# Second chunk's maxima as 16-bit parts made on VectorE, and products in column halves, in the first batch of an mLSTM and Fourier kernel

## Chip, cores and metric

The kernel runs on one core of one Trainium2 chip. The metric is device time in microseconds (us) of an execution of the whole program. The engines are named as the profile names them: PE is TensorE (matrix products, with PEld its weight loads), DVE is VectorE, ACT is ScalarE, POOL is GpSimd, and SP issues DMAs.

## What is computed

An mLSTM cell (batch 4, 8 heads, 768 steps, head size 40) feeds a Fourier mixing layer with a two-layer network. The part that matters here is the recurrence and its running maximum `m`:

```python
for t in range(S):
    kt, vt, qt = (k[:, :, t], v[:, :, t], q[:, :, t])
    m_new = np.maximum(f_gate[:, :, t] + m, i_gate[:, :, t])
    f_stab = np.exp(f_gate[:, :, t] + m - m_new)
    i_stab = np.exp(i_gate[:, :, t] - m_new)
    m = m_new
    C = f_stab[:, :, None, None] * C + i_stab[:, :, None, None] * np.einsum('bhd,bhe->bhde', vt, kt)
    n = f_stab[:, :, None] * n + i_stab[:, :, None] * kt
    h_tilde = np.einsum('bhde,bhe->bhd', C, qt)
    nq = np.einsum('bhd,bhd->bh', n, qt)[:, :, None]
    denom = np.maximum(np.abs(nq), 1.0)
    o = 1.0 / (1.0 + np.exp(-o_gate[:, :, t]))
    y[:, :, t] = o * h_tilde / denom
...
X = np.fft.fft(x, axis=1)
X = np.fft.fft(X, axis=2)
mixed = np.real(X).astype(np.float32)
u = x + mixed
mu = np.mean(u, axis=-1, keepdims=True)
var = np.mean((u - mu) ** 2, axis=-1, keepdims=True)
un = (u - mu) / np.sqrt(var + 1e-06)
ch = np.maximum(un @ w_ch1, 0.0) @ w_ch2
```

## The kernel before

The sequence of 768 steps is cut into six chunks of 128. Inside a chunk the recurrence becomes matrix products: scores of queries and keys (`ps`, line 587), each weighted by an exponential of gate values, then products with the values (`hb`), and a state `C` carried from chunk to chunk (`pc`). Batch 0 is done chunk by chunk, six chunks, while the weights of the network are loaded and converted; batches 1 to 3 run in half chunks among the network's products of the batch before. After its chunks, batch 0 goes through folds on DVE and POOL (lines 892 to 904), the Fourier products over the sequence (`pz`, `hb`, line 970) and over features (`pu`, line 1004), and then into the network.

There is no planner with costs: the order of instructions on each engine is the order in which the program issues them. The function `gates` issues the work of the first microseconds line by line (lines 277 to 302); everything later is put into a plan by slot and phase (`at(slot, phase, ...)`) and is issued in the order of these keys. Engines run their queues in order and wait for each other by semaphores.

What `gates` does for the maxima: the gate arrays are held as 32 rows (batch and head) by chunk and step. `sums` scans the forget gate (`F`), `maxima` subtracts it from the input gate (`a`), copies the carries (`shift`), scans the running maximum (`M`), and makes `nM` and `m_in` of it. This is done for chunk 0 (`first`) and then for chunks 1 to 5 in one go (`others`), all on DVE. `columns` turns `a` (and on a second call `wk`, the weights made by ACT) by PE transposes into columns; both go to one PSUM tile `hb`, and DVE copies them to `colT`.

The exponentials of a chunk need the maximum of each head along the free axis on all 128 partitions. `spread_max` makes them in PSUM for four heads at a time: first a product of the bf16 identity with a triangular mask of large numbers (line 228), then for each head a product that spreads one row (line 233). For chunks 0 and 1 this is an fp32 product of a column of the 128-wide identity with the 128 rows of `Mq` or `M`, so that the rows above 32 have to be zero (line 188). For chunks 2 to 5 it is a bf16 product: `parts` (lines 239 to 243, on POOL) splits each fp32 maximum into three bf16 numbers that add up to it, `M3`, stacked on 96 rows, and `sel` is a stack of three bf16 identities. `mlstm_exp` (line 556, ACT) reads the result. `spread_decay` (line 258) spreads the decays `g`, made by ACT in `decay` (line 267), in the same way in fp32 to the tile `pG`, which DVE multiplies with the queries (`qg`, line 564).

`idle_products` (line 143) are products of zeros whose result nobody reads: three at the start, and two in slot 17, before the folds' products.

## Time and profile before

| | us |
|---|---|
| median of 3 runs | 383.57 |
| the three runs | 384.47, 383.57, 379.48 |
| the profiled execution | 382.09 |
| its span in the profile | 380.2 |

The profiled execution is a run of its own; the span is what the trace covers, 1.9 us less than the device time. All times in what follows are counted from the start of the span. The granted clock of PE is shown as 0.999 over the span. A row of the timeline has start, duration, engine, line, operation, output and inputs, shape, and the number of merged instructions; in brackets stands how long the engine had been idle, and who released it. A product in fp32 appears as two records, one in bf16 as one. A record of PE lasts some 0.2 us beyond the start of the next one, so the pace of products is read from the starts.

The records that belong to the changed lines:

| line, engine | what | records | median of one |
|---|---|---|---|
| 970 PE | `pz`, 128x386 f32 | 10 | 488 ns |
| 970 PE | `hb`, 64x386 f32 | 10 | 513 ns |
| 143 PE | `pi`, 128x256 f32 | 10 | 634 ns |

### The profile page before, as it was taken

How to read it: one execution, taken by the hardware profiler on the slowest of the kernel's cores; microseconds unless marked ns; L12 is line 12 of the kernel's file. 1: busy time of each engine (PE TensorE's matmuls, PEld its weight loads, DVE VectorE, ACT ScalarE, POOL GpSimd, SP SyncE). 2: the span in 40 equal slices, each digit the busy share in tenths (PEclk: the TensorE clock that was granted, in tenths of full speed). 3: DMA queues.
4: the chain of work that ended last, by engine and by line, in shares of the span. 5: the costliest groups of instructions: out<-in, count | busy, mean ns of one | idle time of the engine just before them, and what ended most of it. 6: DMA issues, size and time to landing. Idle time of an engine off the chain costs nothing.

```text
span 380.2 us, 11433 instructions
## 1 busy us (share of the span) xinstructions
PE 373.3 (98%) x4602; PEld 278.2 (73%) x4602; DVE 280.8 (74%) x662; ACT 171.4 (45%) x501; POOL 133.9 (35%) x240
## 2 busy tenths in 40 slices
PE   8999999999999999999999999999999999999996
PEld 6887655567677777666578999676488996546996
DVE  7788999999998585787964787987745885245552
ACT  4878757756442114764442153854520233544000
POOL 5568433775686124471501424561300000020000
PEclk9999999999999999999999999999999999999999
DMA  7978565999870428460002737300000001000011
GB/s 195 284 219 287 168 184 148 252 241 265 278 207 29 127 66 238 134 174 26 0 3 62 205 99 195 102 3 3 0 2 34 17 20 36 0 0 2 34 36 34
DMA packets 20500, 41.93 MB, mean 110 GB/s; under 512 B 3256, under 2 KB 9744, under 8 KB 20320
## 3 DMA queue, kind: packets, MB, share of 16 engines
q1 hardware_dynamic: 20448, 41.21, 37.5%
q8 instruction: 36, 0.59, 0.7%
q14 instruction: 16, 0.13, 0.1%
HBM read 37.10 MB, written 4.10 MB: 108 GB/s over the span
## 4 chain that ended last, share of the span: by engine, by line
PE 79%; DVE 9%; ACT 2%; issue 1%; SPq 1%; POOL 1%; DMA 0%; DVEq 0%; ACTq 0%; POOLq 0%
PE po L1346 22%; PE pm L1217 19%; PE po L1289 8%; PE pm L1134 7%; PE ph L587 5%; PE pm L1151 4%; PE ps L587 4%; PE pu L1004 3%; PE pz L958 2%; PE put L1053 2%; PE pzt L958 1%; PE hb L587 1%; DVE e L480 1%; DVE stats L1027 1%; DVE e L465 1%
## 5 line engine op out<-in xcount | busy, mean ns | idle before, releaser
L1295 DVE SCALAR_TENSOR_TENSOR x<-po,rstd,x 128x160 f32<-128x160 f32 (+1 forms) x69 | 27.1, 394 | 36.3 <-PE po L1346 33.0
L1223 DVE TENSOR_TENSOR h<-h,pm 128x384 f32<-128x384 f32 x60 | 30.5, 550 | 24.2 <-PE pm L1217 11.8
L583 POOL TENSOR_SCALAR_AFFINE_SELECT W<-W 64x512 f32<-64x512 f32 x36 | 28.1, 780 | 37.8 <-ACT W L556 28.8
L1217 PE MATMUL pm<-uT,w_sb 128*128 128x384 f32 x90 | 37.3, 503 | 0.1
L556 ACT ACTIVATE W<-W,colT 128x64 f32<-128x64 f32 x144 | 36.6, 336 | 1.6 <-DMA W<-M_d 1.6
L710 POOL TENSOR_TENSOR C<-C,decB 128x164 f32<-128x164 f32 x33 | 18.1, 549 | 49.4 <-DVE C L717 45.9
L1289 PE MATMUL po<-w_sb,h 128*128 128x320 f32 x120 | 33.6, 432 | 0.0
L1134 PE MATMUL pm<-uT,w_sb 64*64 64x384 f32 x320 | 32.0, 496 | 0.0
L1077 POOL TENSOR_TENSOR t<-rstd 128x6 f32<-128x6 f32 x12 | 3.7, 311 | 76.1 <-DVE v L1071 75.6
L568 POOL TENSOR_TENSOR qg<-qk,Gb 128x512 f32<-128x512 f32 x21 | 28.1, 1337 | 4.5 <-DMA Gb<-G_d 4.2
L1289 PEld LDWEIGHTS po<-w_sb,h 128*128 128x128 f32 x120 | 22.5, 190 | 8.9
L1151 PE MATMUL pm<-uT,w_sb 128*128 128x384 f32 x80 | 28.4, 496 | 0.0
L1346 PE MATMUL po<-T,S 128*128 128x160 f32 x180 | 27.8, 301 | 0.2 <-DVE x L1295 0.2
L1346 PEld LDWEIGHTS po<-T,S 128*128 128x128 f32 x180 | 25.4, 190 | 1.3 <-DVE x L1295 0.4
L1346 PE MATMUL po<-w_sb,h 128*128 128x160 f32 x180 | 26.3, 300 | 0.0
L1346 PEld LDWEIGHTS po<-w_sb,h 128*128 128x128 f32 x180 | 25.2, 190 | 1.4 <-DVE x L1295 0.3
L1217 PEld LDWEIGHTS pm<-uT,w_sb 128*128 128x128 f32 x90 | 15.7, 189 | 12.1 <-DVE h L1223 4.1
L1272 ACT ACTIVATE h<-h 128x384 f32<-128x384 f32 x45 | 23.1, 520 | 2.9 <-DVE h L1223 2.9
L1134 PEld LDWEIGHTS pm<-uT,w_sb 64*64 64x64 f32 x320 | 11.1, 132 | 15.5 <-issue 13.4
L574 POOL TENSOR_TENSOR vw<-kvt,colT 128x328 f32<-128x328 f32 x23 | 19.6, 852 | 7.0 <-DVE colT L290 2.7
L1151 PEld LDWEIGHTS pm<-uT,w_sb 128*128 128x128 f32 x80 | 14.3, 190 | 10.1 <-issue 1.2
L587 PE MATMUL ps<-qk 40*64 40x64 f32 (+1 forms) x768 | 19.9, 240 | 0.3 <-DVE C L717 0.3
(255 smaller groups left out, 825.2 us busy)
## 6 DMA issues: line engine op xcount, KB each, us to landing
kvt<-in_kv SPq DMA_DIRECT2D x24, 336.0 KB
qk<-in_qkT SPq DMA_DIRECT2D x48, 160.0 KB
raw<-in_w SPq DMA_DIRECT2D x10, 640.0 KB
W<-M_d SPq DMA_DIRECT2D x36, 128.0 KB
so<-in_o SPq DMA_DIRECT2D x24, 160.0 KB
out<-x SPq DMA_DIRECT2D x23, 160.0 KB
Gb<-G_d SPq DMA_DIRECT2D x42, 80.0 KB
ds_sb<-in_dft_s SPq DMA_DIRECT2D x1, 1158.0 KB
```

The source lines that it names most:

```text
L556: nc.scalar.activation(out=k.W[:, h, :], in_=M, func=AF.Exp, scale=-1.0, bias=colT[:, c, 0, b * H + h:b * H + h + 1])
L568: nc.gpsimd.tensor_tensor(out=k.qg[:, :, t], in0=k.qk[:, 0, :, t], in1=k.Gb[:, :, t], op=OP.mult)
L583: nc.gpsimd.affine_select(out=W, in_=W, compare_op=OP.is_ge, fill=0.0, base=base, pattern=[[0, H], [-1 if back else 1, LH]], channel_multi ...
L587: nc.tensor.matmul(out, w, x, start=start, stop=True, skip_group_check=True)
L1134: nc.tensor.matmul(banks[i][half(cols)], w1_rest(n)[half(i), half(cols)], u[half(i)], start=start, stop=not start, skip_group_check=True)
L1151: nc.tensor.matmul(k.pm[i], w1_block(ch, f // 2 * 2 + i), u[2 * ch], start=(ch == 0 and not ahead), stop=(ch == 1 and (ahead or n in (2, 5 ...
L1217: nc.tensor.matmul(bank, w, u, start=start, stop=True, skip_group_check=True)
L1223: nc.vector.tensor_tensor(out=h, in0=h, in1=bank, op=OP.add)
L1272: nc.scalar.activation(out=h, in_=h, func=AF.Relu, scale=-1.0)
L1289: nc.tensor.matmul(k.po[m], hidden(gr, f)[:, i * L:(i + 1) * L], w2_sb[:, f, :], start=(f == 0), stop=(f == NFF - 1))
L1295: nc.vector.scalar_tensor_tensor(out=u, in0=po, scalar=k.rstd[:, c:c + 1], in1=u, op0=OP.mult, op1=OP.add)
L1346: nc.tensor.matmul(po, a[:, f], w[:, f], start=start and f == 0, stop=f == half - 1, skip_group_check=True)
```

## The change

It has three parts. First, the maxima of chunk 1 are spread with bf16 products like those of chunks 2 to 5; their parts are made on DVE, right behind the scan of `others`, and the copy of the first chunk's weight columns (`colT[:, first, 1]`) now stands behind them instead of ahead of the scan. The zeros above row 32 of `M[:, 1]` are no longer written, and the zeros of `g` move from DVE to POOL. Second, the two masks of chunk 1 are issued ahead of the decay products, and the eight maxima behind them. Third, the idle products, batch 0's sequence products of line 970 and its feature products of line 1004 (not the row of its own) are issued in column parts: halves, and thirds for the idle ones of slot 17. On ACT and SP nothing changes place.

```diff
+    def columns_of(n, parts):
+        return [slice(i * n // parts, (i + 1) * n // parts) for i in range(parts)]
+
+    def idle_products(n, rest, at_=None, halves=1):
         pw = bank("pi", [L, 2 * L], at_)
         for i in range(n):
-            nc.tensor.matmul(pw, rest[:, 0:L], rest, start=True, stop=True, skip_group_check=True)
+            for cols in columns_of(2 * L, halves):
+                nc.tensor.matmul(pw[:, cols], rest[:, 0:L], rest[:, cols], start=True, stop=True, skip_group_check=True)
...
-        idle_products(3, rest)
+        idle_products(3, rest, halves=2)
...
-        nc.vector.memset(M[:, 1], 0.0)
...
+        nc.gpsimd.memset(g[:, 0:3], 0.0)
...
-        def spread_max(b, c, h0):
+        def spread_mask(b, c, h0):
...
+        def spread_max(b, c, h0):
+
+            k = chunks[b, c]
+            if c != 1:
+                spread_mask(b, c, h0)
             for h in range(h0, h0 + NP):
                 bh = b * H + h
-                w, x = (ident[:, bh:bh + 1], (Mq, M)[c][:, c, :]) if c < 2 else (sel[:, bh:bh + 1], M3[:, c, :])
-                nc.tensor.matmul(k.M[-1][:, h - h0, :], w.to_broadcast([w.shape[0], L]), x, start=False, stop=True,
+                w, x = (sel[:, bh:bh + 1], M3[:, c, :]) if c > 0 else (ident[:, bh:bh + 1], Mq[:, c, :])
+                nc.tensor.matmul(k.M[h0 // NP][:, h - h0, :], w.to_broadcast([w.shape[0], L]), x, start=False, stop=True,
                                  skip_group_check=True)
 
-        def parts(s):
+        def parts(s, eng=nc.gpsimd):
 
-            m, rest_ = (M if s.start == 2 else Mq)[0:BH, s], shift[:, s]
-            nc.gpsimd.tensor_copy(out=M3[0:BH, s], in_=m)
...
+            m, rest_ = (M if s.start < 3 else Mq)[0:BH, s], shift[:, s]
+            eng.tensor_copy(out=M3[0:BH, s], in_=m)
+            eng.tensor_tensor(out=rest_, in0=m, in1=M3[0:BH, s], op=OP.subtract)
+            eng.tensor_copy(out=below[:, s], in_=rest_)
+            eng.tensor_copy(out=M3[BH:2 * BH, s], in_=rest_)
+            eng.tensor_tensor(out=M3[2 * BH:, s], in0=rest_, in1=below[:, s], op=OP.subtract)
...
         mlstm_exp(0, 0, 0)
-        nc.vector.tensor_copy(out=colT[:, first, 1], in_=pt[:, first])
         mlstm_exp(0, 0, NP)
         maxima(others, M[0:BH, 0, L - 1:L])
+        parts(slice(1, 2), nc.vector)
+        nc.vector.tensor_copy(out=colT[:, first, 1], in_=pt[:, first])
         pt = columns(others, 0)
         mlstm_load_o(0, 1)
-        nc.vector.memset(g[:, 0:3], 0.0)
         nc.vector.tensor_copy(out=colT[:, others, 0], in_=pt[:, others])
         decay(slice(1, 2))
         weights(others)
-        spread_max(0, 1, 0)
-        spread_max(0, 1, NP)
+        for h0 in (0, NP):
+            spread_mask(0, 1, h0)
         spread_decay(0, 1)
+        for h0 in (0, NP):
+            spread_max(0, 1, h0)
         pt = columns(others, 1)
...
-        at(17, FILL_PE + 2.7, idle_products, 2, rest, 3)
+        at(17, FILL_PE + 2.7, idle_products, 2, rest, 3, 3)
...
-            nc.tensor.matmul(out, fe[:, p, fm], ds_sb[:, p, i], start=(p == TG - 1), **kw)
+            for cols in columns_of(NK, 2):
+                nc.tensor.matmul(out[:, cols], fe[:, p, fm], ds_sb[:, p, i, cols], start=(p == TG - 1 and cols.start == 0), **kw)
...
-            nc.tensor.matmul(o, z, t, start=(i == 0 or b == 0 and i == 3), stop=(i in (2, 4)), skip_group_check=True)
+            for cols in columns_of(o.shape[1], 2 if b == 0 and i < 3 else 1):
+                nc.tensor.matmul(o[:, cols], z, t[:, cols], start=(cols.start == 0 and (i == 0 or b == 0 and i == 3)),
+                                 stop=(i in (2, 4)), skip_group_check=True)
```

More of the change, by code (lines that the diff above doesn't have):

```diff
@@ L137 @@
     EVAC, FILL, MAIN, FILL_PE = range(4)
-    def idle_products(n, rest, at_=None):
+    def columns_of(n, parts):
+        return [slice(i * n // parts, (i + 1) * n // parts) for i in range(parts)]
+    def idle_products(n, rest, at_=None, halves=1):
         pw = bank("pi", [L, 2 * L], at_)
         for i in range(n):
-            nc.tensor.matmul(pw, rest[:, 0:L], rest, start=True, stop=True, skip_group_check=True)
+            for cols in columns_of(2 * L, halves):
+                nc.tensor.matmul(pw[:, cols], rest[:, 0:L], rest[:, cols], start=True, stop=True, skip_group_check=True)
     def gates(gp):
@@ L229, in spread_max @@
                              skip_group_check=True)
+        def spread_max(b, c, h0):
+            k = chunks[b, c]
+            if c != 1:
+                spread_mask(b, c, h0)
             for h in range(h0, h0 + NP):
                 bh = b * H + h
-                w, x = (ident[:, bh:bh + 1], (Mq, M)[c][:, c, :]) if c < 2 else (sel[:, bh:bh + 1], M3[:, c, :])
-                nc.tensor.matmul(k.M[-1][:, h - h0, :], w.to_broadcast([w.shape[0], L]), x, start=False, stop=True,
+                w, x = (sel[:, bh:bh + 1], M3[:, c, :]) if c > 0 else (ident[:, bh:bh + 1], Mq[:, c, :])
+                nc.tensor.matmul(k.M[h0 // NP][:, h - h0, :], w.to_broadcast([w.shape[0], L]), x, start=False, stop=True,
                                  skip_group_check=True)
-        def parts(s):
-            m, rest_ = (M if s.start == 2 else Mq)[0:BH, s], shift[:, s]
-            nc.gpsimd.tensor_copy(out=M3[0:BH, s], in_=m)
-            nc.gpsimd.tensor_tensor(out=rest_, in0=m, in1=M3[0:BH, s], op=OP.subtract)
-            nc.gpsimd.tensor_copy(out=below[:, s], in_=rest_)
-            nc.gpsimd.tensor_copy(out=M3[BH:2 * BH, s], in_=rest_)
-            nc.gpsimd.tensor_tensor(out=M3[2 * BH:, s], in0=rest_, in1=below[:, s], op=OP.subtract)
+        def parts(s, eng=nc.gpsimd):
[5 more added lines that the diff above has]
+            eng.tensor_tensor(out=M3[2 * BH:, s], in0=rest_, in1=below[:, s], op=OP.subtract)
         def queries():
```

## The prediction

> **What bounds the kernel now.** I read the page first (busy shares), then the chain of waits in order of time, then the timelines of PE and DVE around the change.

> ```profile
> span 380.2 us, 11433 instructions
> PE 373.3 (98%) x4602; PEld 278.2 (73%) x4602; DVE 280.8 (74%) x662; ACT 171.4 (45%) x501; POOL 133.9 (35%) x240
> ```

> PE is nearly always occupied, so whatever takes work or a wait off PE's queue early lets all that follows start earlier, unless another engine or a transfer comes last first. The chain of waits, followed back from the end, can be traced to 19.1 us:

> ```profile
> 19.11 0.11 DVE dec L320
> 19.23 0.04 issue
> 19.26 1.09 PE pG L258 x16
> ```

> From there it runs through PE to 24.3, DVE and POOL to 30.2, PE, ACT to 38.6, DVE nearly without a break to 60, a DMA stretch, and PE alone from about 78. What frees DVE at 19.1 is thus what starts everything after. The timeline of PE before it:

> ```profile
> 7.19 0.61 PE L228 MATMUL pM<-later_r,ident_b 128*128 128x512 bf16 x1
> 7.59 1.91 PE L233 MATMUL pM<-Mq,ident 128*128 128x128 f32 x8
> 9.43 1.76 PE L587 MATMUL ps<-qk 40*64 40x128 f32 x32
> 11.12 0.49 PE L273 MATMUL hb<-ident,a 32*128 32x32 f32 x5
> 11.54 0.39 PE L228 MATMUL pM<-later_b,ident_b 128*128 128x512 bf16 x1
> 11.77 1.05 PE L233 MATMUL pM<-M,ident 128*128 128x128 f32 x8
> 12.66 0.38 PE L228 MATMUL pM<-later_b,ident_b 128*128 128x512 bf16 x1
> 12.88 1.05 PE L233 MATMUL pM<-M,ident 128*128 128x128 f32 x8
> 13.86 1.09 PE L258 MATMUL pG<-x,ident 128*64 128x128 f32 x16
> 14.88 0.49 PE L273 MATMUL hb<-ident,x 32*128 32x32 f32 x5
> 18.04 0.39 PE L233 MATMUL pM<-M,sel 96*128 96x128 bf16 x4
> ```

> No wait stands between 9.43 and 17.9: here PE's own queue is the bound. And DVE in the same stretch:

> ```profile
> 7.29 0.19 DVE L290 COPY colT<-hb 128x32 f32<-128x32 f32 x1 [1.29 <-PE hb L273]
> 7.40 0.80 DVE L210 TENSOR_TENSOR a<-a,F 32x640 f32<-32x640 f32 x1
> 8.13 0.69 DVE L212 COPY shift<-F 32x5 f32<-32x5 f32 x1
> 8.86 1.54 DVE L213 TENSOR_TENSOR_SCAN M<-shift,M,a 32x640 f32<-32x640 f32 x1
> 10.80 0.38 DVE L295 MEMSET x<- 128x384 f32 x1
> 15.42 0.33 DVE L310 COPY colT<-hb 128x160 f32<-128x160 f32 x1 [2.25 <-PE hb L273]
> 15.66 0.48 DVE L465 TENSOR_SCALAR e<-raw 128x640 uint32<-128x640 uint32 x1
> ```

> DVE stands still for 1.29 us behind the column copy of line 290, and again for 2.25 us until PE's transposes of 14.88 are done. After that it is busy without a gap to 19.6, ending with qg of line 564 (18.44, 0.68), whose end frees the bank that PE's pG of 19.26 writes.

> **The products of the second chunk's maxima.** Before, 4 fp32 products take 0.89 us of PE (11.77 to 12.66, and again up to about 13.8). With the bf16 parts, 4 products are worth 0.23 (18.04 to the next mask at 18.27, all in the same PE clock). Two groups: 2 x 0.66 = 1.32 us. The gap of 0.09 between the last fp32 product and pG also goes, since pG now stands right behind the masks. New order from 11.54: two masks 0.45 (0.23 + 0.22), pG 1.02 (13.86 to 14.88), eight products 0.46; together 1.93 against 3.34 before. The transposes of 14.88 come at 13.47: **1.4 us earlier**.

> **The five DVE instructions added.** Their price on DVE is not in the trace for this form. Upper bound: the same five on POOL (line 239 on, 10.47 to 12.44), 1.97 us. Lower: DVE's copy of 32 columns (0.19) and its subtraction of 128 (0.28) give 3 x 0.19 + 2 x 0.28 = 1.1. I take 1.4, nearer DVE's own rows (its copy of 160 columns takes 0.33). They are paid by the scan's move: without line 290 ahead, the subtraction starts at 6.0, when the long sum of 4.54 (1.47) ends, not 7.40. That is 1.4 us earlier; the 0.69 of line 212, a copy of five values beside POOL's vw of 7.57, should shrink too, as vw now waits for the later column copy. I count 0.4. So the maxima are done at about 8.6 instead of 10.40, m_in at 9.0, the parts at 10.3, line 290's copy at 10.5. PE's transposes of 11.12 write the tile that this copy reads, and their wait for DVE is the last one ahead of the products, so it must cover the parts as well: ready 0.6 us early, cost nothing. With 1.97 it is 11.1, still just hidden. If that cover were gone, each microsecond of lateness would be one of the end.

> **What waits behind the later copy.** POOL's vw of the first chunk moves from 7.57 to about 10.6, its own parts for chunk 3 from 10.47 to about 11.7 (ending 13.7). They are wanted by PE at 18.04 less 1.4; vw is wanted by pc at 17.27 less 1.4. Hidden by two to four microseconds. No DMA issue moves on SP past another.

> **The masks ahead, the maxima behind pG.** ACT's exponentials of the chunk started at 12.98, right after its weights. Now decay can start when ACT is free at 10.7 instead of 11.21, but the maxima end at about 13.3, so the exponentials start 0.3 us later, and the chain behind them on ACT (copies, decays of 15.57 on, G_d's issue on SP at 16.88) ends 0.3 later, near 17.2. Who waits: DVE's weighing, at 17.01 less 1.4 = 15.6, its second half at 16.2, against exponentials done at 15.5: free. DVE's dec, at about 17.6: free. PE's heads copy on ACT, 17.48 before, now about 17.15, ahead of px at 20.71 less 1.4: free. The G_d write goes out late by 0.3, but the Gb loads behind it (21.25) feed POOL at 27.31, which DVE released, not they.

> **Memsets.** M's (0.17) leaves DVE before its first input lands; g's (0.38) leaves DVE and costs POOL about as much at 4.9, where POOL is idle until vw. Zero.

> **Column halves.** Ten transform products of 386 columns (line 970) and nine of 321 (line 1004) become two each; the idle ones two at 1.2 us and three at 41.0. In the same stage products of half the width take half the time: the two records of 193 columns of line 967 start 0.17 apart, those of 386 of line 970 0.33. Cost 0 to 0.1 per group of products, nothing taken; what there is hides while DVE is last: the pu products done by about 52.3 are first read by DVE's add at 53.11. Idle thirds: the transposes load 128 weight columns five times in 0.38 us (line 273), so under 0.08 each, near the 0.07 that a third of 0.22 streams. No cost. [...]

> **Sum.** -1.4 on PE's queue at 14.9; DVE's run 15.42 to 19.1 starts 1.4 earlier, with all its inputs there; pG of 19.26 at about 17.9. Everything on the chain after is started by what precedes it. The profiled execution took 382.09 for its span of 380.2, so it becomes 380.7. The median of the three runs is 1.48 higher, 383.57, and becomes 382.2. As the runs lie between 379.48 and 384.47, I put the forecast between the two: **381.4**.

> **Rivals.** *PE is fast earlier in other runs.* In this run the mask takes 0.61 at 7.19 and 0.39 at 11.54: PE went from half to full speed near 10.8. Were it fast from 8.4 on, PE would reach the transposes near 9.9 and wait: before, for the maxima (10.40), now for the parts (10.5). Then the old kernel has its transposes of x at 10.45 + 0.89 + 0.22 + 0.89 + 1.02 = 13.5 and the new one at 10.55 + 0.42 + 1.93 = 12.9: a gain of 0.6 only, 382.2 on the same footing. [...] Chance 0.22.

> *The gain is hidden.* A transfer between 19 and 60 comes last instead. SP's Gb issue of 21.25 stood 0.9 behind G_d's landing and won't move. Against it: POOL's 27.31 and DVE's 24 to 27 were released by engines. Time unchanged, 382.8. Chance 0.18.

> *Slower: the halves pay for their weights.* 19 more products are 38 more records between 42 and 58. If each let 0.1 of its 0.19 us load show, that is 3.8, of which 53.11 - 52.3 = 0.8 hides: +3.0 - 1.4 = +1.6, 384.4. It decides from about 0.06 per record. Against it: 180 records of 160 columns with loads of 190 ns run 0.136 apart (line 1346, x20 in 2.72). Chance 0.06.

> *It doesn't do what it says* (DVE's parts late, PE standing at 11.1): 382 to 383, within the second rival.

> **Numbers.** Forecast 0.50, rivals 0.22, 0.18 and 0.06, 0.04 for what I don't see (such as clock changes in the fold stage). The range of 8 in 10 takes the runs' scatter, some 2 us for a median, and the rivals: 378.6 to 384.2. About 2% (7.7 us) is what a measurement of this kernel can tell from no change; none of the cases reaches it: faster 0.04, within 0.93, slower 0.03.

> **What would show it.** Right: L213's scan near 7.1; five DVE instructions on 32x128 done before 10.6; eight bf16 products in about 0.5 behind pG; DVE's idle before L310 ending near 14; pG of chunk 3 near 17.9, and the same lead at the first products of batch 1 after 60. Wrong: a wait of PE on DVE near 11; ACT idle before the chunk's exponentials growing beyond 1 us; PE later at the transforms than the lead allows; the lead gone by 60.

## The result

Each kernel's time is the median of its executions; the ratio to the kernel before has a 95% interval.

| | median us | lowest to highest | executions |
|---|---|---|---|
| before | 382.93 | 379.48 to 384.47 | 6 |
| changed | 387.34 | 385.41 to 387.78 | 6 |

The ratio is 1.0152 [1.0116, 1.0189]: slower by 4.4 us between the medians, outside the predicted range of 378.6 to 384.2, on the side that had a chance of 0.03 beyond 2% and 0.06 as a rival. The ratios leave out executions over 1.5% above their kernel's fastest; since the cause found below puts executions there, the tables also give the median of all and how many ran with a lowered mean clock (under 0.998).

The profiled execution of the changed kernel took 387.16 us, 5.07 more than that of the kernel before. Its page begins:

```profile
span 385.1 us, 11524 instructions
PE 374.6 (97%) x4646; PEld 283.3 (74%) x4646; DVE 280.2 (73%) x665; ACT 171.5 (45%) x501; POOL 131.5 (34%) x241
```

PE is busy for 1.3 us more in a span that is 4.9 longer: most of the time was lost standing still. Below, "put products" are the products that write the tile `put`, one group for each batch; they mark how far the kernel has come. The timeline of DVE (start, duration, instruction, and in brackets the idle time before it with its releaser):

```profile
6.05 0.81 DVE L214 TENSOR_TENSOR a<-a,F 32x640 f32<-32x640 f32 x1
6.79 0.15 DVE L216 COPY shift<-F 32x5 f32<-32x5 f32 x1
6.98 1.54 DVE L217 TENSOR_TENSOR_SCAN M<-shift,M,a 32x640 f32<-32x640 f32 x1
...
8.71 0.21 DVE L249 CAST M<-M 32x128 bf16<-32x128 f32 x1
...
9.75 0.28 DVE L253 TENSOR_TENSOR M<-shift,below 32x128 bf16<-32x128 f32 x1
10.07 0.19 DVE L303 COPY colT<-hb 128x32 f32<-128x32 f32 x1
```

DVE does what was forecast, slightly sooner: the scan at 6.98, the five parts in 1.32 us (8.71 to 10.03), the column copy at 10.07. The timeline of PE:

```profile
7.40 1.10 PE L599 MATMUL ps<-qk 40*64 40x128 f32 x32
10.32 0.49 PE L283 MATMUL hb<-ident,a 32*128 32x32 f32 x5 [1.81 <-DVE colT L303]
...
11.28 1.76 PE L268 MATMUL pG<-x,ident 128*64 128x128 f32 x16
12.96 1.03 PE L243 MATMUL pM<-M,sel 96*128 96x128 bf16 x8
...
20.06 1.09 PE L268 MATMUL pG<-x,ident 128*64 128x128 f32 x16
```

In this execution PE runs fast from 4.7 us on (the clock records begin with a full clock at 4.72; the scores take 1.10, not 1.76, and are done at 8.5), so the transposes stand for 1.81 us behind the copy of line 303. Then PE is slow: pG takes 1.76 instead of 1.09. The decay products of chunk 3 start at 20.06, not at the forecast 17.9; before it was 19.26. The windows say why (columns: stretch, its length, busy time and count of PE, PEld, DVE, ACT, POOL, granted clock, DMA share, GB/s):

```profile
11.50:18.40 6.90, 6.90 (x81) 5.98 (x79) 3.82 (x7) 3.87 (x15) 5.07 (x10) 0.51 0.89 281
```

By the clock records of the trace, the half clock lasts from 11.55 to 18.37. This early loss of 0.8 us against the profile of before is not the 4.9. By the first put product it has shrunk to 0.27 (55.23 against 54.96), and the scores of 78.04 stood at 77.83 before. The comparison flatters the change, though, for in the profile of before the clock rose only at 10.83. In the halves-only run below, which has the old early part and a clock that rose at 4.54, chunk 3's decay products start like this:

```profile
17.05 0.66 PE L262 MATMUL pG<-x,ident 128*64 128x128 f32 x8 [0.39 <-DVE dec L324]
```

Its first put product stands at 52.75. At the same phase of the clock the changed kernel is thus 3.0 us late at chunk 3 and 2.5 late at put.

The other loss comes later. The changed kernel's chain of waits in order of time (start, duration, what) goes on so:

```profile
78.04 1.00 PE ps L599 x62
79.05 0.11 PE ph L599 x2
79.16 2.78 issue
81.94 0.67 PE ph L599 x27
82.61 6.40 PE pm L1166 x14
```

In the middle of 32 products of one group, PE stands for 2.78 us and waits for nothing that the profile shows: no engine, no transfer of data. In the kernel before, the same products run through:

```profile
78.67 0.68 PE L587 MATMUL ph<-kvt,W 64*64 64x41 f32 x31
```

Right behind the hole the granted clock is 0.50 again, from 83.23 to 86.64; 3.41 us at half the pace are worth 1.7, by an estimate from that clock. 0.2 + 2.8 + 1.7 is 4.7 of the 4.9. Some 0.6 us more are lost near 110 us and won back by 153, untraced. From the second group of put products on (146.89 against 141.37) to the end the two kernels need 238.2 and 238.8 us.

### The profile page after: what moved, and what is told of

Same layout as the page of the kernel before. It is cut to its first block, busy times and chain, and to the rows that moved or that the text cites. A ratio compares the mean times of both kernels' runs of the same rounds, so it can differ in the third digit from the quotient of the medians.

```text
span 385.1 us, 11524 instructions
## 1 busy us (share of the span) xinstructions
PE 374.6 (97%) x4646; PEld 283.3 (74%) x4646; DVE 280.2 (73%) x665; ACT 171.5 (45%) x501; POOL 131.5 (34%) x241
## 4 chain that ended last, share of the span: by engine, by line
PE 84%; DVE 9%; ACT 2%; issue 2%; DMA 1%; POOL 1%; SPq 0%; DVEq 0%; ACTq 0%; POOLq 0%
PE po L1361 22%; PE pm L1232 19%; PE po L1304 8%; PE pm L1149 7%; PE ph L599 5%; PE pm L1166 5%; PE ps L599 4%; PE pu L1018 3%; PE pz L970 2%; PE put L1068 2%; PE hb L599 1%; PE pzt L970 1%; ACT W L568 1%; PE pz L983 1%; DVE stats L1042 1%
## 5 line engine op out<-in xcount | busy, mean ns | idle before, releaser
L1232 PE MATMUL pm<-uT,w_sb 128*128 128x384 f32 x90 | 37.3, 503 | 0.1
L1166 PE MATMUL pm<-uT,w_sb 128*128 128x384 f32 x80 | 30.1, 521 | 0.0
L580 POOL TENSOR_TENSOR qg<-qk,Gb 128x512 f32<-128x512 f32 x21 | 26.9, 1283 | 6.9 <-DMA Gb<-G_d 6.6
L1232 PEld LDWEIGHTS pm<-uT,w_sb 128*128 128x128 f32 x90 | 15.7, 189 | 12.1 <-DVE h L1238 4.1
L1166 PEld LDWEIGHTS pm<-uT,w_sb 128*128 128x128 f32 x80 | 15.1, 199 | 10.8 <-issue 2.9
L1149 PEld LDWEIGHTS pm<-uT,w_sb 64*64 64x64 f32 x320 | 11.1, 132 | 15.5 <-issue 13.4
L586 POOL TENSOR_TENSOR vw<-kvt,colT 128x328 f32<-128x328 f32 x23 | 18.8, 818 | 6.3 <-DVE colT L303 5.2
```

Source lines behind the costliest of these rows:

```text
L580: nc.gpsimd.tensor_tensor(out=k.qg[:, :, t], in0=k.qk[:, 0, :, t], in1=k.Gb[:, :, t], op=OP.mult)
L1149: nc.tensor.matmul(banks[i][half(cols)], w1_rest(n)[half(i), half(cols)], u[half(i)], start=start, stop=not start, skip_group_check=True)
L1166: nc.tensor.matmul(k.pm[i], w1_block(ch, f // 2 * 2 + i), u[2 * ch], start=(ch == 0 and not ahead), stop=(ch == 1 and (ahead or n in (2, 5 ...
L1232: nc.tensor.matmul(bank, w, u, start=start, stop=True, skip_group_check=True)
```

## What the hole is: TensorE's instructions

The transfer list of that stretch holds, besides data, one transfer of instructions:

```profile
q1 hardware_dynamic: 259, 0.80, 93.0%
q8 instruction: 1, 0.02, 2.6%
```

In the whole run there are 36 such transfers of 16 KB on this queue, and 9387 records of PE (products, weight loads, its sequencer's waits), 261 for each transfer: by an estimate from these counts a transfer brings a block of about that many of PE's instructions. If holes are late blocks, they must stand at block edges, a whole number of blocks apart. Two of them in one kernel (the run with the copy first, below) can be counted in a view; it gives PE's products and weight loads up to the first hole and from there to the second:

```profile
0.00:73.50 73.50, 70.45 (x974) 54.75 (x974) 64.55 (x142) 53.95 (x175) 41.48 (x87) 1.00 0.75 222
73.50:79.20 5.70, 4.18 (x126) 2.92 (x127) 5.63 (x10) 2.52 (x8) 3.69 (x5) 1.00 0.83 239
```

126 + 127, and 3 waits of PE's sequencer that this view leaves out: 256. Every hole of PE of over 0.6 us after the first 60 us, in all 17 profiles of this study, counted in the trace by the starts of PE's own records; the wait ahead of PE's last three records (381.74 to 384.58 in the changed kernel) is left out, and "edge before" is the moment at which PE passed the edge one block earlier:

| kernel | start of PE's last record before the hole and of its next, us | PE instructions before it | edge before to transfer's start | transfer's start to PE's next |
|---|---|---|---|---|
| changed | 78.93 to 81.94 | 2241 = 193 + 8 x 256 | 5.16 | 2.58 |
| halves only | 69.62 to 71.66 | 1985 = 193 + 7 x 256 | 1.33 | 2.97 |
| copy first | 72.08 to 74.35 | 1985 | 3.55 | 3.02 |
| copy first | 78.31 to 79.62 | 2241 | 4.63 | 2.91 |
| early, copy first | 83.01 to 85.27 | 2497 = 193 + 9 x 256 | 2.03 | 2.76 |
| before + 52 | 103.38 to 105.13 | 3265 = 193 + 12 x 256 | 3.58 | 2.67 |
| before + 128 | 93.83 to 94.80 | 3009 = 193 + 11 x 256 | 4.61 | 2.73 |
| halves + 80 | 85.33 to 87.47 | 2753 = 193 + 10 x 256 | 4.20 | 2.72 |
| early, copy first + 16 | 83.75 to 85.50 | 2497 | 4.85 | 2.90 |
| changed + 92 | 88.97 to 90.44 | 2753 | 4.83 | 2.67 |
| copy first + 92 | 79.17 to 82.76 | 2497 | 4.87 | 2.98 |
| halves, half weights | 76.72 to 78.98 | 2241 | 6.67 | 2.66 |

## The experiments

**1. The parts of the change, and the copy's place.** Early change alone: all products whole.

```diff
-        idle_products(3, rest, halves=2)
+        idle_products(3, rest)
...
-        at(17, FILL_PE + 2.7, idle_products, 2, rest, 3, 3)
+        at(17, FILL_PE + 2.7, idle_products, 2, rest, 3)
...
-            for cols in columns_of(NK, 2):
+            for cols in columns_of(NK, 1):
...
-            for cols in columns_of(o.shape[1], 2 if b == 0 and i < 3 else 1):
+            for cols in columns_of(o.shape[1], 1):
```

> The changed kernel with every product whole again (start, fold stage, transforms): the early change alone. Supply theory (the 5 us are one hole of 3.0 us in TensorE's instruction stream at 78.9 us, where nothing that the profile shows is waited for and an instruction transfer starts inside the hole, and the half clock that follows it from 83.2 to 86.6): the early change alone puts other instructions at that place, so the hole goes or moves; 381 to 383.5 if the profile has no such hole, 386 to 388 if it has one. Early-idle theory (the wait of TensorE for the column copy, 1.8 us to 10.3, and the half clock from 11.5 to 18.4 lose the time): both are still there, so 386 to 388. Halves theory (column halves cost TensorE time in the fold stage and the transforms): 382 to 383.

Halves only: the kernel before with those column loops and nothing else.

> The kernel before with all column halves and thirds and nothing of the early change. Supply theory: 382.5 to 384 (the thirds of the fold stage are 0.45 us longer by the changed kernel's trace) without a hole, 386 to 388 with one. Early-idle theory: TensorE keeps its full clock from 10.8 us, so 382.5 to 384 for the thirds alone. Halves theory: 386 to 388, as the changed kernel.

Copy first: the changed kernel with two lines exchanged.

```diff
+        nc.vector.tensor_copy(out=colT[:, first, 1], in_=pt[:, first])
         parts(slice(1, 2), nc.vector)
-        nc.vector.tensor_copy(out=colT[:, first, 1], in_=pt[:, first])
```

> The changed kernel with the column copy put back ahead of the five part instructions (behind the scan), so that TensorE's transposes need not wait for the parts. Early-idle theory: TensorE's wait ends at 8.9 instead of 10.3, the clock does not fall at 11.5, the decay products of the third chunk start near 18.0 instead of 20.06, and the end falls by 3 to 5 to 382 to 384. Supply theory: the start is earlier by as much, and the time falls below 384 only if the hole at 79 us is gone as well. Halves theory: at most 1 us of gain.

Both, early change with the copy first and whole products:

> As the run before, and with every product whole again. Early-idle theory: 381 to 383. Supply theory: 380.5 to 383 without a hole of over 2 us in TensorE's stream, 386 to 388 with one. Halves theory: 381 to 382.5, and less than the run before by the price of the halves.

The kernel before was at 380.69 in these runs, with a lowered clock in 2 of 19.

| | median us | ratio of the comparison | lowered clock in |
|---|---|---|---|
| early change alone | 382.74 | 1.0042 [1.0016, 1.0067] | 7 of 10 |
| halves only | 384.35 | 1.0121 [1.0057, 1.0184] | 4 of 4 |
| changed, copy first | 384.31 | 1.0107 [1.0067, 1.0147] | 3 of 4 |
| early, copy first | 381.99 | 0.9996 [0.9958, 1.0035] | 4 of 10 |

The parts add up: 1.0042 x 1.0121 = 1.0164, beside 1.0152 for the whole. The halves cost about 4 us; the late copy 0.45%, 1.7 us, with halves or without. The two differences behind these 0.45% (with halves, and without) are each about as large as their interval; their agreement is what speaks for them. No single one of the three theories had foreseen both, and each missed some of its times. The supply theory's 381 to 383.5 for the early change without a hole held, but with a hole it had named 386 to 388, and the halves alone have one of 1.55 us at 384.35, the early change with the copy first one of 2.03 at 381.99. It needed a test by instruction count.

**2. Moving the edges alone.** Tiny products whose results nobody reads were put behind the idle products of the fold stage:

```diff
+    def small_products(n, ident_b):
+        pw = bank("pi", [L, 2 * L], 3)
+        for i in range(n):
+            o = slice(i % 2 * LH, i % 2 * LH + LH)
+            nc.tensor.matmul(pw[o, 0:8], ident_b[0:LH, 0:LH], ident_b[0:LH, 0:8], start=True, stop=True, skip_group_check=True)
...
+        at(17, FILL_PE + 2.71, small_products, 52, ident_b)
```

> The kernel before with 52 tiny products (64x64 weights, 8 columns, 104 TensorE instructions, results never read) behind the idle products of the fold stage, and no halves: as many instructions more as all column halves add. Block theory (TensorE takes its instructions in blocks of 256; every hole of the traces so far stands exactly at instruction 193 + 256 n, and what matters is where such a boundary falls in the bursts of the stage from 66 to 90 us): the boundary 1729 falls into the burst at 69 us as in the halves-only kernel, 2.0 us are left for a transfer that needs 2.7 us and its queueing, so a hole of 1 to 3 us near 70 to 72 us in the profile and a median 3 to 5 us above the kernel before. Halves theory (the halved products themselves cost the time): within 1 us of the kernel before.

> As the run before with 128 tiny products, 256 instructions, one whole block: more work added, but the boundaries fall on the same products as in the kernel before. Block theory: within 1.5 us of the kernel before and 2 us or more faster than the run with 52. If the tiny products cost by their number (or by their time): slower than the run with 52.

> All column halves and thirds on the kernel before (as in the halves-only run) with 80 tiny products: 104 and 160 instructions, 8 more than one block. Block theory: the 4.6 us that the halves cost fall to 0.5 to 2 us, near 381 to 382.5 where the kernel before is at 380.7. Halves theory: as the halves-only run, 384 to 385, or more.

> The early change with the column copy ahead of the parts, all products whole, and 16 tiny products: 15 instructions more than the kernel before instead of 17 less, where by the trace of the kernel before the smallest time between two boundaries from 60 to 110 us is 3.9 instead of 2.5 us. Block theory: fewer holes, 0.5 to 1.5 us below the kernel without the 16 products, so 379 to 380.5 where the kernel before is at 380.7. Otherwise: as without them, within 0.4% of the kernel before.

And later on the changed kernel itself:

> The changed kernel, all of it, with 92 tiny products in the fold stage: 87 and 184 instructions, 15 more than one block. Block theory: the part of its loss that the halves cost goes (about 4 us), the part of the late column copy stays (1.7 us): 382 to 384 where the kernel before is at 380.9. If the halves themselves cost the time: 386 to 388.

> The changed kernel with the column copy ahead of the parts and the same 92 tiny products. Block theory together with the early-idle theory: both losses gone, 380 to 382. If either cause is something else: 383 or more.

The kernel before was at 380.92 in the first four runs and at 380.79 in the other two, with a lowered clock in 5 and 9 of 35.

| | median us | ratio | lowered clock in |
|---|---|---|---|
| before + 52 | 383.65 | 1.0043 [1.0008, 1.0078] | 8 of 12 |
| before + 128 | 383.34 | 1.0072 [1.0039, 1.0105] | 11 of 12 |
| halves + 80 | 381.62 | 1.0019 [0.9987, 1.0052] | 1 of 12 |
| early, copy first + 16 | 381.03 | 0.9977 [0.9940, 1.0013] | 2 of 12 |
| changed + 92 | 383.02 | 1.0044 [1.0005, 1.0083] | 3 of 12 |
| copy first + 92 | 382.74 | 1.0035 [1.0005, 1.0064] | 4 of 12 |

The third row decides: with 160 instructions *more*, which bring the edges back to within 8 instructions of where the kernel before has them, the halves cost 0.19% instead of 1.21%. The changed kernel falls to 1.0044 the same way, which is what the late copy alone cost. 52 tiny products without any halves bring 2.7 us by the medians, 0.43% by the ratio, and a hole. That they only shift the later stages in time is excluded for the profiled pair: both clocks rise at 10.83, the first put products stand at 55.09 and 54.96, and from there the run is less than 0.2 us behind the kernel before, record for record, until its hole at 103, which adds 1.4. Several expectations missed. The 52 stayed under their 3 to 5 us, and the hole came at 103 us and not at 70. The 128 were meant as harmless and were not: they take 2.19 us at 40.03, and the clock halves for 3.41 us at 42.35, so that run shows their own price and nothing of the edges. And the copy with 92 stayed 0.7 above its bound; its profile still has a hole of 3.1, so the 92 did not exclude a hole; executions with a lowered clock went from 3 of 4 to 4 of 12. The version with 16 was forecast at 379 to 380.5 and came to 381.03. It has the lowest ratio of the study, but its interval holds 1: no version was shown to beat the kernel before.

**3. Less load traffic.** Of each weight piece, only a part of the columns was loaded and read repeatedly, so the other weights are not the reference's; first half of them, then an eighth:

```diff
-            nc.sync.dma_start(out=self.raw, in_=self.src)
+            nc.sync.dma_start(out=self.raw[:, 0:n // 8], in_=self.src[:, 0:n // 8])
...
-            self.lo, self.hi = words[:, :, 0], words[:, :, 1]
+            self.lo, self.hi = (words[:, 0:n // 8, i].unsqueeze(1).to_broadcast([L, 8, n // 8]) for i in range(2))
```

> The kernel before with only the first half of the columns of each int64 weight piece loaded and used twice (so the weights of the second halves are not the reference's): 0.32 MB instead of 0.64 MB per piece in the transfer queues, TensorE's instructions unchanged. It is the measure for the next run; by itself it may gain what the loads cost, 0 to 3 us.

> The halves-only kernel with the same half loads of the weight pieces. Block theory (a block's transfer waits behind the loads that are queued before it, up to 6 us in the stage from 66 to 90, and with less ahead of it it comes in time): the 1.2% that the halves cost fall to 0.5% or less against the run before this one, and the instruction transfers of the stage start sooner after their boundary. If the transfer's lateness has nothing to do with the loads: still 1.0 to 1.4% above it.

> The kernel before with only the first eighth of the columns of each int64 weight piece loaded, and used eight times (other weights than the reference's): 0.08 instead of 0.64 MB per piece; TensorE's instructions as before. The measure for the next run. Loads theory (block transfers wait behind loads): DMA share from 66 to 90 us falls to 0.7 or less, block transfers of the stage start within 2 us of their boundary; 378.5 to 380.5. If the wait has another source: their delays stay at 2 to 6 us.

> The halves-only kernel with the same eighth of the weight loads. Loads theory: the place where only 2.0 us lie between two boundaries (69 us) still cannot be met when a block takes 2.7 us, so a hole of up to 1 us there, but the others go: 0 to 1 us above the run before this one by the medians of all executions, instead of 3.7 with whole and half loads. If the wait has another source: 3 us or more above it, with holes of 2 us.

| weights loaded | before, median us | halves only, median us | difference | before, ratio | halves only, ratio |
|---|---|---|---|---|---|
| all | 380.69 | 384.35 | 3.7 | 1 | 1.0121 [1.0057, 1.0184] |
| half | 380.64 | 384.34 | 3.7 | 0.9987 [0.9951, 1.0022] | 1.0048 [1.0010, 1.0085] |
| an eighth | 381.20 | 381.04 | -0.2 | 1.0012 [0.9986, 1.0037] | 1.0031 [1.0000, 1.0062] |

The ratios are to the kernel before in the same set of runs, and each row is a set of its own. The half settles little: by the medians the halves cost as much as before, by the ratios 0.6%, where 0.5% or less was expected. The stage from 66 to 90 us stayed full (DMA share 0.80 in the halves), and one block's transfer started 6.67 us after its edge. Yet this pair of profiles shows most plainly where the loss lies. Both clocks rise at 5.3, both first put products stand at 53.01, and record for record the products after the transforms stay within 0.1 us of each other until the hole at 76.72. The hole and the half clock behind it (80.34 to 83.75) put the halves 4.0 us back, and by 4.0 they end later (spans of 377.8 and 381.8).

With an eighth the windows of the same stage read, before first and halves second:

```profile
66.00:90.00 24.00, 23.73 (x481) 14.81 (x481) 23.27 (x42) 15.96 (x51) 17.60 (x22) 1.00 0.79 207
```

```profile
66.00:90.00 24.00, 23.72 (x509) 14.66 (x511) 22.95 (x42) 15.06 (x46) 18.83 (x24) 1.00 0.71 184
```

PE is busy for all but 0.3 us in both, at full clock. With all the weights the halves had:

```profile
66.00:90.00 24.00, 22.45 (x472) 13.94 (x471) 20.38 (x38) 12.46 (x38) 16.53 (x20) 0.93 0.92 250
```

The DMA share did not fall as far as expected (0.79 and 0.71 against 0.7). In the halves the transfers for the edges from 69 to 97 us start within 0.9 to 2.0 us. In the kernel before they do not come sooner, on the whole, than with all the weights: that of 70.39 starts after 3.16 us, against 2.77 for the one of 70.56, and its time did not fall to the expected 378.5 to 380.5. So it is shown that the halves cost next to nothing once the loads are small; that a block waits in the queues behind loads fits this, but rests on one profile of the halves. By the ratios (1.0031 against 1.0012) 0.2% is left, and 3 of 12 executions still had a lowered clock. Which loads a block would wait behind was not separated.

**4. The early loss: wait or clock.** Early change alone, with idle products in the wait:

```diff
+        idle_products(3, rest, 3)
         pt = columns(others, 0)
```

> The early change with whole products (column copy behind the parts, as in the changed kernel) and three idle products of TensorE in the wait for that copy. If the loss is the fall of the clock: no half clock between 11 and 18.5 us in any phase, the decay products of the third chunk near 17.5 (copy at 10.1) and 0.5 to 1.5 us less than the early change alone. If it is the wait: as the early change alone, near 382 to 383 where the kernel before is at 380.7.

Measured: 380.99, with the kernel before at 381.29 in these runs; ratio 1.0010 [0.9974, 1.0047], beside 1.0042 without. In its profile, with the clock up from 4.9 as in the changed kernel's:

```profile
8.44 1.56 PE L147 MATMUL pi<-rest 128*128 128x256 f32 x6
10.34 0.49 PE L283 MATMUL hb<-ident,a 32*128 32x32 f32 x5 [0.34 <-DVE colT L303]
...
11.30 1.09 PE L268 MATMUL pG<-x,ident 128*64 128x128 f32 x16
...
17.52 1.09 PE L268 MATMUL pG<-x,ident 128*64 128x128 f32 x16 [0.66 <-ACT so L668]
```

The transposes start as late as in the changed kernel, but pG keeps its 1.09 and chunk 3's starts at 17.52 instead of 20.06: these 2.5 us go with the half clock, which lasts from 11.55 to 18.37 there and is missing here. With the copy first it starts at 16.34 when the clock is up that early: the 1.2 more go with the wait. This split is read from single profiles; the ratios with and without the idle products have intervals that overlap.

## Why the prediction was wrong

**The price of the parts and the scan's move** were right: 1.32 us for 1.4, the scan at 6.98 for 7.1.

**The saving of 1.4 on PE** is there, under the prediction's condition and with the copy first. Where the clock rises near 10.7, as in the profile of before, pG of chunk 3 starts at 17.94 instead of 19.26, 1.3 earlier; where it rises near 4.7, at 16.34 instead of 17.05, 0.7 earlier, as the rival "PE is fast earlier" put it (0.6). In profiles without a hole a lead is kept, up to 0.8: from the first put product to the second group it is 86.4 us in the kernel before, 86.5 in the early change alone, 87.2 in that with filled wait. The time itself does not show the gain: with the copy first and whole products the ratio is 0.9996 [0.9958, 1.0035], where 1.4 us would be 0.9963. The profiled execution of that run loses its lead in a hole at 83 us.

**The column copy behind the parts** is the first step that failed: "ready 0.6 us early, cost nothing". It held for an execution whose PE is slow until 10.8. Of 17 profiles in this study only 4 had that; in 12 the clock rose between 4.3 and 5.8, in one at 7.5. There PE reaches the transposes at 8.5 and the cover is gone. The rival had this condition but counted only the smaller gain, not the wait of 1.8, nor the 6.8 us of half clock that came behind it (11.55 to 18.37). The prediction's own sentence, each microsecond of lateness is one of the end, would have priced the wait; the 2.5 us that go with the half clock come on top. In the place of "nothing" the runs put 0.45%, 1.7 us.

**"Column halves. Cost 0"** is the second and larger one. Their pace was right: from the first pz product to the first pu it is 6.92 us in both kernels (42.68 to 49.60, 43.68 to 50.60). The rival in which halves pay for their weights named 384.4, near the 384.35 of the halves alone, but that is luck, for its cause is one that the runs exclude: with edges put back, or with less load traffic, they cost 0.7 us or nothing. What failed is the assumption that instructions which hide where they stand are free. They shift all later ones against the edges, here by 104. In the place of 0 the runs put 1.21%, some 4 us. The idle thirds were mis-sized: 1.57 us (line 147, at 41.84) against 1.13 (line 143, at 41.05), so 0.44 more, where the prediction had no cost.

**The gain is hidden**, as a rival, expected an unchanged time because a transfer comes last. By the reading of the holes a transfer did come last, but one of instructions, and its hole of 2.78 us is more than the gain of 1.4.

## What to carry to other kernels

Count the instructions that an edit adds ahead of a dense stage, not only their time: here 104 of them went with 1.21%, and with 160 further ones it was 0.19%. When a hole in mid-group waits for nothing that the profile shows, count the engine's instructions up to it and look for an instruction transfer near it: all twelve holes here stood a whole number of blocks of 256 apart, and PE went on 2.6 to 3.0 us after such a transfer began. And before an order is justified by "the other engine is late anyway", look at more than one execution: in the 17 profiles here TensorE's clock rose at times from 4.3 to 10.8 us.

## What had not been expected of the hardware

All eight falls of TensorE's granted clock in the 17 profiles, those at the end of the program left out, came at the end of a period of 3.41 us counted from the clock's rise (83.23 is 23 periods of 3.413 after 4.72). In seven of these periods PE stood for 1.5 to 2.1 us: 1.55 in the halves alone, 1.99 in the early change with the copy first. The eighth, at 42.35 behind the 128 tiny products, came without such idleness: PE's records cover 4.24 of the 4.30 us from 38.0 to 42.3. Nor does such idleness always bring a fall: 1.78 inside one period (copy first) brought none, and neither did a hole of 3.1 us (copy first + 92), though 1.92 of it lay in one period. So these runs show no rule. In these profiles a fall lasted one period (3.41 us, as from 83.23 to 86.64), or two (6.83 us) after the waits of 1.8 and 1.9 at 8.5 us.
